# Turning part of the normed rows by transposing transfers, and moving steps of the opening, in a fused attention and SwiGLU kernel

## The chip, the cores and the metric

The kernel runs on one core of one Trainium2 chip. The metric is the device time of one execution in microseconds. Before the change it is 336.01 us, the median of 3 runs (335.22 to 336.15). A core has five engines with a queue of their own each: TensorE (PE; weight loads are shown as PEld), VectorE (DVE), ScalarE (ACT), GpSimd (POOL) and SyncE (SP), which here only issues transfers.

## The reference

Attention with a hash mask, then a SwiGLU block on its output:

```python
q_bucket, k_bucket = ...   # 6 sign bits of q @ proj and k @ proj
scores = where(q_bucket == k_bucket, q @ k.T / sqrt(64), -1e9)
attn = softmax(scores) @ v                       # 4 batches, 8 heads, 768 tokens, 64 columns
x = attn, heads side by side                     # 3072 rows of 512
xn = x / sqrt(mean(x * x, axis=-1) + 1e-6) * rms_g
g = xn @ w_gate                                  # 512 x 1536
out = (g * sigmoid(g) * (xn @ w_val)) @ w_out    # 1536 x 512
```

## The kernel before, in words

**Slots.** The work is written out by hand as 192 slots (`SLOTS`). A slot is one pair of score blocks: a half batch `w` (0 to 7, 384 queries), a head `h`, and a third `p` of the keys. Half batches 0 and 1 are the two halves of batch 0, and so on. In each slot `s` the program writes the scores of slot `s + 1` (L344), the exponential of these (L354, ACT), and whatever `at(slot, step, ..., rank=)` has put into slot `s`, lower ranks first; ranks under 3 come ahead of the exponential. This order is the order of every engine's queue: nothing is rearranged later. An engine waits at an instruction until its operands are there, and what is behind it waits too.

**Attention.** Loads of k, q and v come in pairs of heads `(b, hp)` into one pool of buffers (`lpool`, L62). The rows of k and q have to be turned so that the 64 columns lie on partitions. The pairs in `BY_PE` (batch 0 and pair (1, 0)) are turned by TensorE (`keep_pair`, L170, with a copy out of PSUM, L178); the others by VectorE in 32 x 32 blocks (`turn_dve`, L194), for which the k and q loads are cut into pieces of 32 columns (`load_blocks`, L122). Casts to fp16 follow (L186, L202). A hash (`hash_one`, `hash_pair`, `hash_lone`, `hash_pairs`; L210) makes sign bits (L217), which are moved below the turned rows in tile QK, by VectorE (L250, L270) or by SP's transfers (L248, L268, L285, L303). Scores need rows and bits. Probabilities times v are L366 (`av`), in two halves in the second and third slot after the head's last one. v is copied by `v_prep` (L310); its mean (`v_mean`, L325) is added to the output (L381). The output is normed with the reciprocal of its sum (L386, L390).

**SwiGLU.** For each half batch `w`: the squares are summed (L402, L406), `norm(w)` (L413 to L419) gives the factor `rstd`, `scale_x(w, c)` (L424, VectorE) scales chunk `c` of 128 rows, and `turn_x(w, c)` turns it: four transposes on TensorE into one PSUM bank (L431), then a product on VectorE with the gain column `gcol` into `xnT` (L432). Gates (L446), values (L456) and the output product (L469) follow: gates of `w` start at slot `s0 = 24 * w + 42`, the output products at `s0 + 16`. `bank` hands out three PSUM banks in turn to all of this: hash, turns, means, gates, values and outputs.

**SP's queue.** SP issues almost all loads, bit moves and outputs in program order. Each of its transfers also waits until the one eight places earlier has landed.

Of the kernel before, what the change touches and what calls it, by code (L numbers as in the profile page):

```python
# [8 lines left out]
FP32 = mybir.dt.float32  # L9
FP16 = mybir.dt.float16  # L10
AF = mybir.ActivationFunctionType
ALU = mybir.AluOpType
# [6 lines left out]
DMODEL = H * D  # L19
# [18 lines left out]
LAST = {(w, h): g for g, (w, h, p) in enumerate(SLOTS) if p == 2}  # L38
# [2 lines left out]
BY_PE = [(0, hp) for hp in range(4)] + [(1, 0)]  # L41


@with_exitstack
def kernel(
    ctx: ExitStack,
# [11 lines left out]
    nc = tc.nc  # L58
    PSUM = bass.MemoryType.PSUM

    const = ctx.enter_context(tc.tile_pool(name="const", bufs=1))
    lpool = ctx.enter_context(tc.tile_pool(name="lpool", bufs=10))  # L62
    tpool = ctx.enter_context(tc.tile_pool(name="tpool", bufs=2))
    qkpool = ctx.enter_context(tc.tile_pool(name="qkpool", bufs=6))
    ppool = ctx.enter_context(tc.tile_pool(name="ppool", bufs=3))
# [17 lines left out]
    scl = const.tile([128, 1], FP32, name="scl")  # L83
    mhalf = const.tile([128, 3], FP32, name="mhalf")
    gcol = const.tile([128, 4], FP32, name="gcol")
    wg = const.tile([128, 4, DFF], FP16, name="wg")
    wv = const.tile([128, 4, DFF], FP16, name="wv")
    wo = const.tile([128, NF, DMODEL], FP16, name="wo")
# [4 lines left out]
    def bank(name, shape=None, dt=FP32):  # L93
        return gps.tile(shape or [128, 512], dt, name=name, tag="g")
# [237 lines left out]
    x, ssp, xn, xnT, ht = {}, {}, {}, {}, {}  # L332
# [76 lines left out]
    rstds = {}  # L409
# [11 lines left out]
    def scale_x(w, c):  # L421
        if w not in xn:
            xn[w] = npool.tile([128, 3, DMODEL], FP16, name="xn")
        nc.vector.tensor_scalar_mul(xn[w][:, c, :], x[w][:, c, :], rstds[w][:, c : c + 1])  # L424

    def turn_x(w, c):
        if w not in xnT:
            xnT[w] = npool.tile([128, 4, HALF], FP16, name="xnT", bufs=2)
        ps = bank("x_ps", [128, 4, 128], FP16)
        for kt in range(4):  # L430
            nc.tensor.transpose(ps[:, kt, :], xn[w][:, c, kt * 128 : (kt + 1) * 128], ident16)  # L431
        nc.vector.tensor_mul(  # L432
            xnT[w][:, :, c * 128 : (c + 1) * 128], ps,
            gcol.unsqueeze(2).to_broadcast([128, 4, 128]),
        )
# [89 lines left out]
    def load_wo(f0, f1):  # L525
# [2 lines left out]
            in_=moe_w_out[f0 * 128 : f1 * 128, :].rearrange("(k p) n -> p k n", p=128),  # L528
        )

    def columns_of_proj():
        rows = pn.unsqueeze(1).to_broadcast([128, 4, 6])
        for t, sign in ((pk, 1.0), (pq, -1.0)):
            nc.vector.scalar_tensor_tensor(
                out=t[:, 0:24].rearrange("p (c n) -> p c n", n=6), in0=pm, scalar=sign,
                in1=rows, op0=ALU.mult, op1=ALU.mult,
            )
# [14 lines left out]
    keep(nc.scalar, 0, 0, "q")  # L552
    cast_half(0, 0, "q", 0, nc.scalar)
    columns_of_proj()
    idle(wz[:, 0:128], 5)
    bits0 = hash_head(0)
# [19 lines left out]
    def at(s, f, *a, rank=3):  # L576
        plan[s].append((rank, len(plan[s]), lambda: f(*a)))
# [17 lines left out]
        at(1 + h, cast_half, 0, h, "q", 1)  # L595
        at(h, (bits0, bits1)[h], (nc.vector,), 3)

    for hp, turns, sv in ((1, (1, 2, 4, 5), 8), (2, (7, 8, 9, 10), 17), (3, (12, 13, 14, 15), 22)):
        for i, s in enumerate(turns):
            at(s, keep_pair, 0, hp, i)  # L600
            at(s + 1, casts, 0, hp, i)
        at(sv, v_prep, 0, hp)

    for h, s in ((2, 3), (3, 7)):
        at(s, hash_one, h)
        for t in range(3):
            at(s + 1 + t, lambda h=h, t=t: moves[h]((nc.vector,), t), rank=5)
    for hp, s, slots in ((2, 12, (13, 14, 15, 16)), (3, 17, (18, 19, 20, 21))):
        at(s, hash_pair, 0, hp)
        for i, s in enumerate(slots):  # L610
            at(s, lambda hp=hp, i=i: moves[0, hp](nc.vector, [divmod(i, 2)]), rank=5)
    for hp, s in enumerate((6, 16, 22, 29)):
        at(s, v_mean, 0, hp, 2, range(6))
    for i, (t, src) in enumerate(((wg, moe_w_gate), (wv, moe_w_val))):
        at(2 + 4 * i, load_w, t, src, 0, 768)
        at(12 + 9 * i, load_w, t, src, 768, 1536)
        at(31 + 21 * i, load_wo, 6 * i, 6 * i + 6)


    for which, sl in zip("kqv", (9, 11, 15)):  # L620
        at(sl, load_rows, nc.sync, 1, 0, which)
    for i, sl in enumerate((23, 25, 27, 29)):
        at(sl, keep_pair, 1, 0, i)
        at(sl + 1, casts, 1, 0, i)
    at(31, hash_pair, 1, 0)
    at(27, v_prep, 1, 0)
    for h in range(2):
        at(41 + h, cast_half, 1, h, "q", 0)
# [4 lines left out]
    def in_row(loads, s, hash_slot=None):  # L633
        return loads, range(s, s + 8), (s + 4, s + 8, s + 9), hash_slot

    work = {
        (1, 1): in_row((21, 22, 32), 42, 51), (1, 2): in_row((32, 33, 37), 49, 58),
        (1, 3): in_row((38, 40, 44), 56, 65),
        (2, 0): in_row((53, 55, 58), 64), (2, 1): in_row((59, 62, 66), 72, 81),
        (2, 2): in_row((68, 71, 75), 81), (2, 3): in_row((78, 82, 86), 89, 98),  # L640
        (3, 0): in_row((90, 94, 98), 100), (3, 1): in_row((100, 104, 108), 110, 119),
        (3, 2): in_row((116, 120, 124), 126), (3, 3): in_row((126, 130, 134), 136, 145),
    }
    for (b, hp), (loads, turns, cast_slots, sh) in work.items():
        for which, s in zip("kqv", loads):
# [11 lines left out]
        at(cast_slots[2], v_sum, b, hp)  # L657
        if b > 1 and hp % 2:
            at(48 * b + (17 if hp == 3 else -4), v_mean, b, hp - 1, 4)
    for hp, s in enumerate((48, 62, 69, 78)):  # L660
        at(s, v_mean, 1, hp, 2)

    gts, sqs = {}, {}
# [13 lines left out]

    for w in range(8):
        for h in range(H):
            end = LAST[w, h] + 3  # L680
            at(end - 1, av, w, h, 0, 9)
            at(end, av, w, h, 9, 18)
            if h % 2:
                at(end, o_step, w, h // 2, rank=4.5)
                if (w, h) != (0, 7):
                    late = 3 if h == 7 and w < 3 else 5 if (w, h) == (0, 5) else 4
                    at(end + late, s_step, w, h // 2, rank=5 if late != 5 else 4)
        s0 = 24 * w + 42
        n0 = {0: 9, 2: 7}.get(w, 11)
        at(s0 - n0, norm, w, rank=5)  # L690
        for c in range(3):
            at(s0 - {0: 5 - c // 2, 2: 6 - c}.get(w, 8 - c), scale_x, w, c, rank=5)
            xs = {0: (3, 2, 1), 2: (4, 2, 1)}.get(w, (5, 3, 1))
            at(s0 - xs[c], turn_x, w, c, rank=1)
        seen = set()
        for ft in range(NF):
            for f, s in ((g_step, s0 + 16 * ft // NF), (v_step, s0 + (32 * ft + 16) // (2 * NF))):
                at(s, f, w, ft, rank=4 if s in seen else 2)
                seen.add(s)
        for i in range(9 if w < 7 else 6):  # L700
            c, j = divmod(i, 3)
            at(s0 + 16 + i, project, w, c, 4 * j, 4 * j + 4, rank=1 if i == 8 else 3)


    for s in range(NS + 48):
# [3 lines left out]
        n = sum(r < 3 for r, _, _ in todo) if s < NS - 1 else 0  # L709
# [54 lines left out]
```

## Time and profile before

| | |
|---|---|
| median of 3 runs | 336.01 us |
| profiled execution | 334.87 us, span 333.1 us |
| granted TensorE clock | 0.999 |
| busy: PE / DVE / ACT / POOL | 324.1 / 237.9 / 207.8 / 155.6 us |
| DMA | 31.36 MB, 94 GB/s on average |

The profile shows one execution. A row of a timeline has the start, the time until the end of the last of the merged instructions, the engine, the line, the operation, the tiles written and read, the number of instructions merged, and in brackets how long the engine was idle before and what ended that. `SPq` are issues of transfers on SP: their time is that of the issue, waits between them included, not that of the transfer. Matmuls are pipelined: the distance from one start to the next is what they cost.

### The profile page before, as it was taken

The page shows a single profiled execution, that of the slowest core. Times are in us where ns is not written, and L with a number is a line of the kernel's source. Part 1 is how long each engine was busy: PE and PEld are TensorE (multiplying, and loading weights), DVE is VectorE, ACT ScalarE, POOL GpSimd, SP SyncE. Part 2 cuts the span into 40 slices and gives each one's busy share as a digit, 9 for nine tenths or more (in the row PEclk, how much of TensorE's full clock was granted, in tenths as well). Part 3 has the DMA queues.
Part 4 walks back from the last instruction along what each step waited for, and adds up shares of the span by engine and source line. Part 5 has one row for each costly group of instructions (what it writes and reads, how often), then busy time and mean ns, then how long its engine had stood idle before and what let it go on. Part 6 is the DMA issues. An engine that isn't in the chain of part 4 may idle for free.

```text
span 333.1 us, 7797 instructions
## 1 busy us (share of the span) xinstructions
PE 324.1 (97%) x2983; PEld 199.3 (60%) x2983; DVE 237.9 (71%) x532; ACT 207.8 (62%) x324; POOL 155.6 (47%) x230
## 2 busy tenths in 40 slices
PE   8999989999989999999999999999999999999995
PEld 6566666555556556565566656566666656655653
DVE  4789669998588976789577785967357753793860
ACT  3789887665566666657576766657666766422421
POOL 5888955587666665737644364643110311130000
PEclk9999999999999999999999999999999999999999
DMA  7999999887649528308240751000100001002002
GB/s 218 355 229 207 159 138 147 146 143 104 138 83 171 100 49 213 46 18 153 102 81 15 147 128 63 3 16 4 65 33 0 3 31 65 2 1 83 13 0 94
DMA packets 85972, 31.36 MB, mean 94 GB/s; under 512 B 71480, under 2 KB 82992, under 8 KB 85936
## 3 DMA queue, kind: packets, MB, share of 16 engines
q1 hardware_dynamic: 82000, 26.09, 34.3%
q0 software_dynamic: 3712, 4.72, 8.8%
q8 instruction: 23, 0.38, 0.5%
q14 instruction: 13, 0.11, 0.1%
q10 hardware_dynamic: 224, 0.07, 0.1%
HBM read 28.32 MB, written 6.29 MB: 104 GB/s over the span
## 4 chain that ended last, share of the span: by engine, by line
PE 83%; DVE 7%; DMA 4%; POOL 2%; ACT 1%; issue 1%; SPq 0%; DVEq 0%; POOLq 0%; ACTq 0%
PE y_ps L469 18%; PE v_ps L456 16%; PE s_ps L344 15%; PE g_ps L446 14%; PE o_ps L366 8%; PE d_ps L210 4%; PE s_ps L446 4%; DMA wo<-in_moe_w_out_dram 2%; DMA QK<-bits 2%; PE x_ps L431 1%; PE t_ps L170 1%; PE z_ps L337 1%; PE y_ps L721 1%; DVE t L457 1%; DVE otmp L381 1%
## 5 line engine op out<-in xcount | busy, mean ns | idle before, releaser
L354 ACT ACTIVATE psb<-s_ps 128x768 f16<-128x768 f32 x192 | 150.6, 809 | 29.6 <-PE s_ps L344 27.9
L344 PE MATMUL s_ps<-QK 76*128 76x384 f16 x384 | 93.6, 325 | 2.2 <-ACT psb L354 0.9
L456 PE MATMUL v_ps<-xnT,wv 128*128 128x384 f16 x384 | 78.1, 326 | 0.0
L469 PE MATMUL y_ps<-wo,ht 128*128 128x512 f16 x276 | 69.4, 379 | 0.1
L448 ACT ACTIVATE t<-g_ps 128x384 f32<-128x384 f32 x78 | 38.2, 490 | 46.3 <-PE g_ps L446 45.7
L366 PEld LDWEIGHTS <-psb 128*128 128x128 f16 x1152 | 52.2, 97 | 21.8 <-issue 3.7
L457 DVE SCALAR_TENSOR_TENSOR t<-t,g_ps 128x384 f32<-128x384 f32 x78 | 42.7, 547 | 31.0 <-ACT t L448 30.4
L446 PE MATMUL g_ps<-xnT,wg 128*128 128x384 f16 x312 | 63.4, 325 | 1.2 <-DVE xnT L432 0.6
L390 POOL TENSOR_TENSOR x<-otmp,rcp 128x384 f32<-128x384 f32 x31 | 25.9, 835 | 79.3 <-DVE rcp L386 78.8
L458 DVE SCALAR_TENSOR_TENSOR ht<-t,v_ps 128x384 f16<-128x384 f32 x96 | 53.2, 554 | 10.5 <-PE v_ps L456 1.1
L366 PE MATMUL o_ps<-vl,psb 128*128 128x65 f16 x1152 | 56.7, 193 | 0.0
L446 PEld LDWEIGHTS <-wg 128*128 128x128 f16 x384 | 36.0, 97 | 25.1 <-issue 1.7
L456 PEld LDWEIGHTS <-wv 128*128 128x128 f16 x384 | 36.2, 97 | 23.4 <-issue 0.3
L344 PEld LDWEIGHTS <-QK 76*128 76x128 f16 x384 | 31.4, 98 | 19.9 <-issue 6.8
L469 PEld LDWEIGHTS <-ht 128*128 128x128 f16 x276 | 25.8, 97 | 25.1 <-issue 1.6
L476 ACT COPY ysb<-y_ps 128x512 f32<-128x512 f32 x23 | 13.5, 586 | 25.3 <-PE y_ps L469 24.9
L402 POOL TENSOR_TENSOR sq<-x 128x384 f32<-128x384 f32 x31 | 25.7, 828 | 2.5
L202 POOL CAST QK<-qT 64x768 f16<-64x768 f32 x22 | 18.2, 827 | 18.0 <-DVE qT L194 17.3
L432 DVE TENSOR_TENSOR xnT<-x_ps,gcol 128x512 f16<-128x512 f16 x24 | 16.2, 681 | 14.2 <-PE x_ps L431 14.2
L381 DVE TENSOR_TENSOR otmp<-o_ps,cvb 128x390 f32<-128x390 f32 x32 | 17.9, 558 | 8.2 <-PE o_ps L366 8.1
L202 POOL CAST QK<-kT 64x768 f16<-64x768 f32 x22 | 18.2, 828 | 10.5 <-PE v_ps L456 4.0
L194 DVE STREAM_TRANSPOSE kT<-kL 128x192 f32<-128x192 f32 x44 | 22.1, 517 | 0.0
(80 smaller groups left out, 300.0 us busy)
## 6 DMA issues: line engine op xcount, KB each, us to landing
vL<-in_v_dram SPq DMA_DIRECT2D x16, 384.0 KB
out_dram<-ysb SPq DMA_DIRECT2D x23, 256.0 KB
kL<-in_k_dram SPq DMA_DIRECT2D x44, 96.0 KB
qL<-in_q_dram SPq DMA_DIRECT2D x44, 96.0 KB
kL<-in_k_dram SPq DMA_DIRECT2D x4, 384.0 KB
qL<-in_q_dram SPq DMA_DIRECT2D x4, 384.0 KB
wg<-in_moe_w_gate_dram POOLq DMA_DIRECT2D x2, 768.0 KB, 8.6
wv<-in_moe_w_val_dram POOLq DMA_DIRECT2D x2, 768.0 KB, 9.1
```

What stands on the lines that cost most here:

```text
L202: nc.gpsimd.tensor_copy(QK[b, hp][0:64, hh, o : o + S], T0[b, hp, which][64 * hh : 64 * hh + 64, :])
L344: nc.tensor.matmul(ps[:, j, 0:HALF], k_cols(w // 2, h, 2 * p + j), q_cols(w, h), start=True, stop=True,)
L354: nc.scalar.activation(psb[w, h][:, p], sps.pop(g)[:, :, 0:HALF], AF.Exp, scale=ESCALE,)
L366: nc.tensor.matmul(o[:, c, hh, 0:65], psb[w, h][:, jt // 2, jt % 2, 128 * c : 128 * c + 128], vls[b % 2][:, h, v_chunk(b, h, jt), 0:65], s ...
L390: eng.tensor_mul(xd.rearrange("p c (h d) -> p c h d", h=2), tmp[:, :, :, 0:64], r.to_broadcast([128, 3, 2, 64]),)
L402: nc.gpsimd.tensor_mul(sq, xd, xd)
L446: nc.tensor.matmul(g, wg[:, kt, fs], xnT[w][:, kt], start=(kt == 0), stop=(kt == 3))
L448: nc.scalar.activation(t, g, AF.Tanh, scale=0.5)
L456: nc.tensor.matmul(vv, wv[:, kt, fs], xnT[w][:, kt], start=(kt == 0), stop=(kt == 3))
L457: nc.vector.scalar_tensor_tensor(out=t, in0=t, scalar=1.0, in1=g, op0=ALU.add, op1=ALU.mult)
L458: nc.vector.scalar_tensor_tensor(out=ht[w][:, ft], in0=t, scalar=0.5, in1=vv, op0=ALU.mult, op1=ALU.mult)
L469: nc.tensor.matmul(y, ht[w][:, ft, c * 128 : (c + 1) * 128], wo[:, ft, :], start=(ft == 0), stop=(ft == NF - 1),)
```

## The change

Two things are changed together.

First, the turning of the normed rows. For half batches 3, 4 and 5 and chunks 0 and 1 of the three, `turn_x` no longer uses TensorE. Four transposing transfers on SP write the turned blocks straight from `xn` to `xnT`. As no VectorE product follows, `scale_x` multiplies by the gain too, from a new tile `grow`, the gain broadcast to all partitions, which one load at slot 78 fills. Scaling and transfers of these chunks are put at slots `s0 - 9` and `s0 - 8`; the third chunk is turned as before. For the new tile `lpool` has 9 buffers instead of 10.

Second, slots. In the opening: head 3's k is turned at slot 3 instead of 4, the hash of head 2 at 4 instead of 3, the turns of pair (1, 0) at 20, 21, 24, 27 instead of 23, 25, 27, 29, its hash at 33 instead of 31, the last mean of batch 0 at 30 instead of 29. For half batch 0, the last head's `av` and what follows it come one slot earlier, the norm two, the scalings at `s0 - 6`, and the turns one earlier. Later: loads of (1, 2), (2, 0) to (2, 2), (3, 1) and (3, 3) and two means of batch 1 are moved.

```diff
+BY_DMA = (3, 4, 5)
-    lpool = ctx.enter_context(tc.tile_pool(name="lpool", bufs=10))
+    lpool = ctx.enter_context(tc.tile_pool(name="lpool", bufs=9))
+    grow = const.tile([128, DMODEL], FP32, name="grow")
 ...
     def scale_x(w, c):
-        nc.vector.tensor_scalar_mul(xn[w][:, c, :], x[w][:, c, :], rstds[w][:, c : c + 1])
+        if w in BY_DMA and c < 2:
+            nc.vector.scalar_tensor_tensor(
+                out=xn[w][:, c, :], in0=x[w][:, c, :], scalar=rstds[w][:, c : c + 1],
+                in1=grow, op0=ALU.mult, op1=ALU.mult,
+            )
+        else:
+            nc.vector.tensor_scalar_mul(xn[w][:, c, :], x[w][:, c, :], rstds[w][:, c : c + 1])
 
     def turn_x(w, c):
+        if w in BY_DMA and c < 2:
+            for kt in range(4):
+                nc.sync.dma_start(
+                    out=xnT[w][:, kt, c * 128 : (c + 1) * 128],
+                    in_=xn[w][:, c, kt * 128 : (kt + 1) * 128], transpose=True,
+                )
+            return
 ...
+    def load_grow():
+        nc.sync.dma_start(
+            out=grow, in_=moe_rms_g.rearrange("(o n) -> o n", o=1).to_broadcast([128, DMODEL])
+        )
 ...
-    for hp, turns, sv in ((1, (1, 2, 4, 5), 8), (2, (7, 8, 9, 10), 17), (3, (12, 13, 14, 15), 22)):
+    for hp, turns, sv in ((1, (1, 2, 3, 5), 8), (2, (7, 8, 9, 10), 17), (3, (12, 13, 14, 15), 22)):
-    for h, s in ((2, 3), (3, 7)):
+    for h, s in ((2, 4), (3, 7)):
-    for hp, s in enumerate((6, 16, 22, 29)):
+    for hp, s in enumerate((6, 16, 22, 30)):
         at(s, v_mean, 0, hp, 2, range(6))
+    at(78, load_grow)
-    for i, sl in enumerate((23, 25, 27, 29)):
+    for i, sl in enumerate((20, 21, 24, 27)):
         at(sl, keep_pair, 1, 0, i)
-    at(31, hash_pair, 1, 0)
+    at(33, hash_pair, 1, 0)
 ...
     work = {
-        (1, 1): in_row((21, 22, 32), 42, 51), (1, 2): in_row((32, 33, 37), 49, 58),
+        (1, 1): in_row((21, 22, 32), 42, 51), (1, 2): in_row((34, 35, 37), 49, 58),
-        (2, 0): in_row((53, 55, 58), 64), (2, 1): in_row((59, 62, 66), 72, 81),
-        (2, 2): in_row((68, 71, 75), 81), (2, 3): in_row((78, 82, 86), 89, 98),
-        (3, 0): in_row((90, 94, 98), 100), (3, 1): in_row((100, 104, 108), 110, 119),
-        (3, 2): in_row((116, 120, 124), 126), (3, 3): in_row((126, 130, 134), 136, 145),
+        (2, 0): in_row((53, 55, 59), 64), (2, 1): in_row((66, 67, 68), 72, 81),
+        (2, 2): in_row((71, 74, 77), 81), (2, 3): in_row((78, 82, 86), 89, 98),
+        (3, 0): in_row((90, 94, 98), 100), (3, 1): in_row((99, 101, 112), 110, 119),
+        (3, 2): in_row((116, 120, 124), 126), (3, 3): in_row((126, 127, 137), 136, 145),
     }
 ...
-    for hp, s in enumerate((48, 62, 69, 78)):
+    for hp, s in enumerate((48, 60, 64, 78)):
         at(s, v_mean, 1, hp, 2)
 ...
-            end = LAST[w, h] + 3
+            end = LAST[w, h] + (2 if (w, h) == (0, 7) else 3)
 ...
-        n0 = {0: 9, 2: 7}.get(w, 11)
+        n0 = {0: 11, 2: 7}.get(w, 11)
         at(s0 - n0, norm, w, rank=5)
         for c in range(3):
-            at(s0 - {0: 5 - c // 2, 2: 6 - c}.get(w, 8 - c), scale_x, w, c, rank=5)
-            xs = {0: (3, 2, 1), 2: (4, 2, 1)}.get(w, (5, 3, 1))
-            at(s0 - xs[c], turn_x, w, c, rank=1)
+            scale, rank = {0: 6, 2: 6 - c}.get(w, 8 - c), 1
+            turn = {0: (4, 3, 2), 2: (4, 2, 1)}.get(w, (5, 3, 1))[c]
+            if w in BY_DMA and c < 2:
+                scale, turn, rank = 9 - c, 9 - c, 6
+            at(s0 - scale, scale_x, w, c, rank=5)
+            at(s0 - turn, turn_x, w, c, rank=rank)
```

## The prediction

> **What bounds the kernel now.** I read the page's shares first, then busy time by stretches of the span.
>
> ```profile
> span 333.1 us, 7797 instructions
> PE 324.1 (97%) x2983; PEld 199.3 (60%) x2983; DVE 237.9 (71%) x532; ACT 207.8 (62%) x324; POOL 155.6 (47%) x230
> ```
> ```profile
> 28.00:32.00 4.00, 3.44 (x50) 2.34 (x47) 3.78 (x9) 3.49 (x6) 2.87 (x6) 1.00 1.02 230
> 38.00:42.00 4.00, 3.64 (x54) 2.01 (x51) 2.69 (x7) 3.22 (x5) 3.35 (x6) 1.00 1.16 188
> 42.00:48.50 6.50, 5.64 (x83) 3.98 (x80) 4.95 (x16) 5.94 (x9) 3.15 (x5) 1.00 1.11 168
> 90.00:105.00 15.00, 14.05 (x134) 8.83 (x133) 12.86 (x30) 9.52 (x16) 7.99 (x11) 1.00 0.61 133
> 127.00:166.00 39.00, 38.86 (x358) 23.48 (x357) 30.46 (x66) 25.16 (x39) 23.10 (x32) 1.00 0.46 103
> ```
>
> The columns are stretch, length, then busy time of PE, PEld, DVE, ACT and POOL, the granted clock and the DMA share. TensorE is the bound. From 127 to 166 us it has 0.14 us of holes, at full clock. There a matmul fewer is time saved, and a late operand is time lost at once. In the opening, up to 48.5 us, holes remain, but ACT (5.94 of 6.50) and DVE (3.78 of 4.00) are nearly as full, so that not every hole can be closed. The last place with holes is 90 to 105 us. TensorE's timeline names what ended each hole, in its last bracket:
>
> ```profile
> 12.44 0.83 PE L210 MATMUL d_ps<-kT,pk 128*32 128x384 f32 x2 [0.41 <-DVE kT L178]
> 29.82 0.48 PE L344 MATMUL s_ps<-QK 76*128 76x384 f16 x2 [0.30 <-POOL QK L186]
> 31.26 0.48 PE L344 MATMUL s_ps<-QK 76*128 76x384 f16 x2 [0.26 <-ACT psb L354]
> 41.49 0.49 PE L344 MATMUL s_ps<-QK 76*128 76x384 f16 x2 [0.36 <-ACT psb L354]
> 43.64 0.48 PE L344 MATMUL s_ps<-QK 76*128 76x384 f16 x2 [0.25 <-ACT psb L354]
> 48.49 0.81 PE L446 MATMUL g_ps<-xnT,wg 128*128 128x384 f16 x4 [0.58 <-DVE xnT L432]
> 94.43 0.81 PE L446 MATMUL g_ps<-xnT,wg 128*128 128x384 f16 x4 [0.47 <-DVE t L457]
> 96.56 0.48 PE L344 MATMUL s_ps<-QK 76*128 76x384 f16 x2 [0.39 <-DMA QK<-bits]
> ```
>
> The profiled execution took 334.87 us (span 333.1), the median of the runs is 336.01, so 1.14 us above it. I make the sum against 334.87 and add 1.14 at the end.
>
> **1. Opening: hash of head 2 from slot 3 to 4, the turn of head 3's k from 4 to 3.** The hash is the matmul at 12.44 that waited 0.41 us for VectorE's copy. Now a turn and a score pair stand ahead of it, work that was to be done anyway. I take 0.4 us.
>
> **2. First norm.** The second half of head 7's probabilities times v comes one slot earlier, the norm two, the three scalings at slot 36 instead of 37, 37 and 38, the turns one slot earlier each; the hash of (1, 0), whose matmuls stood ahead of this chain, goes behind it. The gate's wait of 0.58 us goes. Price: nothing new is issued, and the norm's small operations find POOL waiting for VectorE:
>
> ```profile
> 43.49 0.19 POOL L415 TENSOR_SCALAR ms<-ss 128x3 f32<-128x3 f32 x1 [2.08 <-DVE ss L413]
> ```
>
> I take 0.6 us.
>
> **3. Turns of (1, 0) to slots 20, 21, 24, 27 and its hash to 33.** They put TensorE work into slots in which it waited for ACT or POOL (0.30, 0.26, 0.36 and 0.25, together 1.17 us) and take it out of fuller ones. ACT must keep up:
>
> ```profile
> 40.63 7.36 ACT L354 ACTIVATE psb<-s_ps 128x768 f16<-128x768 f32 x10 [0.36 <-PE s_ps L344]
> ```
>
> From 40.63 to 48 it runs ten exponentials with no pause, at 0.73 us each ((7.36 - 0.81)/9 with a last one of 0.81), so that part can't be shortened, only be entered earlier; the pause ahead of it, 0.36, and ACT's share of 3.49 in 4.00 before 32 us leave room. I take half of the 1.17: 0.6 us; bounds 0 and 1.2. Two k casts on POOL now come ahead of the copy of v of (0, 3); its mean is one slot later for that. Opening together: 1.6 us (0 to 2.2).
>
> **4. Second stage, 90 to 105 us.** The 0.47 at 94.43 follows the mean of (1, 2) at slot 69, which holds one of three PSUM banks in the middle of gates; it moves to slot 64, ahead of them. The 0.39 at 96.56 is a wait for bits. Their signs were ready at 86.42, but on SP they stood behind loads and an output:
>
> ```profile
> 85.74 0.68 DVE L217 TENSOR_SCALAR bits<-d_ps,thr,scl 128x384 f16<-128x384 f32 x1
> ...
> 99.47 0.54 DVE L194 STREAM_TRANSPOSE kT<-kL 128x192 f32<-128x192 f32 x1
> ```
> ```profile
> 85.89 2.85 SPq L122 DMA_DIRECT2D kL<-in_k_dram  x4
> 88.84 0.58 SPq L478 DMA_DIRECT2D out_dram<-ysb  x1
> 89.47 2.67 SPq L122 DMA_DIRECT2D qL<-in_q_dram  x4
> 92.91 7.05 SPq L285 DMA_DIRECT2D QK<-bits  x8
> ```
>
> The change puts those k and q loads at slots 66 and 67, behind the bits, which can then go at 86.4 instead of 92.9. What is late next: these loads themselves. Bits to about 93.5 (7.05 us), an output 0.58, k 2.85, then 1.84 of landing (row below) is 98.8; VectorE needs the k rows at 99.47 less what is gained before, which moves SP's start as well. So the margin is some tenths. I take 0.8 of the 0.86.
>
> The eight other moved loads and the pool of nine buffers instead of ten cost nothing: the tile nine places back is read some slots ahead of each load, with one exception, the load of v of (0, 3) in the opening, which now waits for the turn of head 3's k (near 12 us) on SP; its v is needed near slot 22. The broadcast load of the gain (256 KB, once, at slot 78) is one more SP issue, some 0.5 us, ahead of a k load due eleven slots later.
>
> **5. Turns by transfers, w = 3, 4, 5.** Removed from TensorE: 3 x 2 x 4 = 24 transposes. Their price is the distance of starts:
>
> ```profile
> 157.25 0.39 PE L431 MATMUL x_ps<-ident,xn 128*128 128x128 f16 x4
> 157.48 1.03 PE L469 MATMUL y_ps<-wo,ht 128*128 128x512 f16 x4
> ```
>
> Four take 0.23 us (their 218 ns each overlap), so six groups take 1.4 us, in a stretch without holes. I take 1.3, with what may be hidden. VectorE loses six of these products (the first row) and gets six scalings with the gain in a two-input form, like the third row:
>
> ```profile
> L432 DVE TENSOR_TENSOR xnT<-x_ps,gcol 128x512 f16<-128x512 f16 x24 | 16.2, 681 | 14.2 <-PE x_ps L431 14.2
> L424 DVE TENSOR_SCALAR xn<-x,rstd 128x512 f16<-128x512 f32 x24 | 15.4, 668 | 2.9 <-POOL rstd L419 2.9
> L458 DVE SCALAR_TENSOR_TENSOR ht<-t,v_ps 128x384 f16<-128x384 f32 x96 | 53.2, 554 | 10.5 <-PE v_ps L456 1.1
> ```
>
> That is 554 x 512/384 = 739 ns instead of 668: 0.4 us more and 4.1 less, on an engine that is not the bound.
>
> Added: 24 transposing transfers on SP, 8 per half batch, between a scaling at slots s0 - 9 and s0 - 8 and the first gate at s0. The trace has no such transfer. So I work out the room and then what price fits it.
>
> ```profile
> 152.63 2.71 SPq L122 DMA_DIRECT2D qL<-in_q_dram  x4
> ...
> 190.02 2.71 SPq L122 DMA_DIRECT2D qL<-in_q_dram  x4
> 195.83 0.35 SPq L478 DMA_DIRECT2D out_dram<-ysb  x1
> ```
> ```profile
> 165.99 0.81 PE L446 MATMUL g_ps<-xnT,wg 128*128 128x384 f16 x4
> 203.97 0.81 PE L446 MATMUL g_ps<-xnT,wg 128*128 128x384 f16 x4
> 242.49 0.81 PE L446 MATMUL g_ps<-xnT,wg 128*128 128x384 f16 x4
> ```
> ```profile
> 193.08 1.02 DVE L424 TENSOR_SCALAR xn<-x,rstd 128x512 f16<-128x512 f32 x1
> ```
> ```profile
> 227.44 0.86 POOL L419 TENSOR_TENSOR rstd<-ms,mhalf 128x3 f32<-128x3 f32 x1
> ```
> ```profile
> 94.59 1.84 DMA QK<-bits
> ```
>
> For w = 3 the q load of (3, 1), now at slot 101, still ends on SP at 155.34, since SP works without pause there; the scaled rows are ready by then. The gate comes at 165.99 - 0.45 (the turns that are gone); its fourth matmul, which needs the last transfer, 0.49 later. So 165.99 - 0.45 + 0.49 - 155.34 = 10.7 us of room. For w = 4: 203.97 + 0.04 - 192.73 = 11.3 (the first scaling, at 193.08 before, is a slot earlier and done near 192.8: 11.2). For w = 5, SP is idle, the norm is ready at 227.44 + 0.86 = 228.3 and the scaling done near 229.6: 12.9. With a landing of 1.84 us, as in the last row, eight transfers at x us each (by SP's issue or by the queue, whichever is slower) fit when 8x + 1.84 is under 10.7: x up to 1.11 us. Each tenth above costs 0.8 us per half batch.
>
> Nearest rows for x: an output of 128 rows takes 0.35 us of SP, a k load of 32 partitions with 768 short pieces 2.85/4 = 0.71, a bit row 7.05/8 = 0.88. From below 0.35. From above nothing is certain: pieces at 2.71/(4 x 768) = 0.88 ns each, an estimate, would make 16,384 single elements 14.4 us. A turned block of 128 rows has to be cut finer than an output, but no reason in the trace makes it elementwise; I take the price near the short-piece load, 0.7 to 0.9, so 8x + 1.84 is 7.4 to 9.0 us and no gate waits. SP's next work, the outputs of the half batch before and the loads of v, is late by at most some us, and three output buffers cover that until the next half batch, 24 slots on.
>
> The Trainium skill, VectorE: DVE Perf Modes, section The three transpose paths, lists 390 ns for TensorE and 1309 ns for the transfer of a 128 x 128 block. By its 390 the removed turns would be worth 24 x 0.39 = 9.4 us; the starts above say 1.4. If its 1309 is what each costs in a row, x is above the limit: waits of 1.6 and 1.1 us, and the sum 335.0 instead of 332.3. Its page Advanced Engine Details and Errata, section X-Bar Transpose (TRN2), says instead that such transfers are as fast as plain ones, which is the forecast. No row here decides between them.
>
> **Sum.** 334.87 - 1.6 - 0.8 - 1.3 = 331.2; with 1.14 it is 332.3, said as 332.4.
>
> **Rivals.**
> - *Transfers a little dear.* x of 1.11 to 1.42. SP's dearest four loads took 1.4 us each, while DMA was full:
>
> ```profile
> 36.37 5.50 SPq L122 DMA_DIRECT2D qL<-in_q_dram  x4
> ```
>
> At 1.41 the waits at the three gates are 2.4, 1.9 and 0.2 us, together 4.5: 336.8. In the middle 335.
> - *Transfers dear: slower.* One mechanism: PE stands at the first gate of w = 3, 4 and 5 for the last transfer. From x = 1.42 us the three waits exceed 4.7 us and eat all gains; at 2 us they are 7.1, 6.6 and 4.9 and the time is 351. For it: the trace shows no transfer that turns, and the scaling was put nine slots ahead. Against: every SP row but those with full rings is under 0.9 us.
> - *The moved slots give nothing.* ACT and DVE at 90% and more take the opening's holes back, and VectorE waits at slot 72 for the late k rows: only step 5 is left, 336.01 - 1.3 = 334.7, up to 336.5 with waits of that kind.
>
> **Chances.** A difference under 0.3% (1.0 us) can hardly be told from none here. Forecast 0.48 (331 to 334); a little dear 0.13 (0.06 faster, 0.04 same, 0.03 slower); dear 0.20, slower; slots give nothing 0.19 (0.07 faster, 0.07 same, 0.05 slower). Faster 0.61, same 0.11, slower 0.28. The range goes from 330.8, all holes named closed, to 338.5, which is x near 1.5; what lies beyond is most of the dear case.
>
> **What would show it.** Right: SP's transposing issues near 0.7 to 0.9 us each and no wait of g_ps for DMA in front of w = 3, 4, 5; no 0.58 at the first gate, which starts near 46.9 instead of 48.49; no 0.47 and 0.39 near 93; 24 transposes fewer. Wrong: PE g_ps waiting for DMA xnT, or for ACT and POOL in the opening as long as before, or DVE's L194 waiting for kL near 96.

## The result, and the profile after

The changed kernel took 337.84 us, the median of 22 runs (336.84 to 339.39); before, on the same chip, took 336.22 (22 runs, 335.12 to 339.58). The ratio is 1.004, with a 95% interval of 1.0021 to 1.0059: about 1.3 us slower. The prediction said 332.4, faster; the time lies in its range, near the upper end, but on the slower side of before.

The page of after begins so (columns as before):

```profile
span 336.0 us, 7784 instructions
PE 324.2 (96%) x2959; PEld 198.1 (59%) x2959; DVE 233.7 (70%) x526; ACT 208.2 (62%) x324; POOL 156.4 (47%) x230
```

The 24 transposes are gone from TensorE (2983 to 2959), and six products from VectorE, yet the span is 2.9 us longer. Busy time by stretches says where TensorE stands:

```profile
90.00:105.00 15.00, 14.22 (x138) 9.13 (x137) 12.28 (x30) 10.05 (x18) 7.87 (x11) 1.00 0.62 121
127.00:166.00 39.00, 38.84 (x351) 23.10 (x349) 28.95 (x64) 25.17 (x39) 23.47 (x32) 1.00 0.41 84
166.00:169.00 3.00, 1.43 (x8) 0.76 (x8) 0.00 (x0) 0.96 (x2) 0.82 (x1) 1.00 0.34 113
204.00:208.00 4.00, 3.04 (x24) 1.49 (x21) 0.32 (x2) 1.13 (x3) 1.26 (x3) 1.00 0.32 101
244.00:247.00 3.00, 2.43 (x14) 1.19 (x13) 0.20 (x1) 1.30 (x3) 0.00 (x0) 1.00 0.44 156
```

The stretch from 127 to 166 us is as full as it was. Three short stretches behind it are not, and each lies at the first gate of one of the half batches 3, 4 and 5. The waits of TensorE over the whole span, longest sum first (us, times, longest):

```profile
PE g_ps L463 <- DMA xnT<-xn: 2.4, 3, 0.9
...
PE v_ps L473 <- DVE t L474: 0.8, 1, 0.8
PE g_ps L463 <- ACT ysb L493: 0.7, 1, 0.7
PE x_ps L448 <- DVE xn L434: 0.5, 1, 0.5
```

The first row is the one the prediction named as its refutation. TensorE's timeline at these gates:

```profile
166.65 0.69 PE L463 MATMUL g_ps<-xnT,wg 128*128 128x384 f16 x3 [0.68 <-ACT ysb L493]
168.26 0.32 PE L463 MATMUL g_ps<-xnT,wg 128*128 128x384 f16 x1 [0.92 <-DMA xnT<-xn]
...
207.10 0.32 PE L463 MATMUL g_ps<-xnT,wg 128*128 128x384 f16 x1 [0.90 <-DMA xnT<-xn]
...
245.91 0.34 PE L463 MATMUL g_ps<-xnT,wg 128*128 128x384 f16 x1 [0.57 <-DMA xnT<-xn]
```

A gate is four matmuls, one for each block of 128 columns; the last of them (x1) needs the last transfer, and all four need chunk 1. At 166.65 the first three had waited too. The row names ACT's copy `ysb`, which ended just then (166.01 and 0.59). The transfers didn't end this wait: by the trace's records of landings, the blocks that the first two matmuls need were there at 164.34 and 165.61. Why the gate waits for that copy stays open; in `e3_one_chunk`, with fewer transfers, and in `e4_room`, with eight, the same gate starts ahead of the same copy.

```profile
164.96 0.81 PE L463 MATMUL g_ps<-xnT,wg 128*128 128x384 f16 x4
```
```profile
165.16 0.58 ACT L493 COPY ysb<-y_ps 128x512 f32<-128x512 f32 x1 [1.80 <-PE y_ps L486]
```

For the sum it makes no difference: the fourth matmul starts at 168.26, when the last transfer has landed (168.22), whatever the first three do, so the whole delay of this gate is the transfers'. Against the usual distance of starts, TensorE loses 2.0, 1.3 and 0.7 us at the three gates, 4.0 in all. The other side is SP's timeline:

```profile
152.89 2.71 SPq L126 DMA_DIRECT2D qL<-in_q_dram  x4
155.79 11.28 SPq L441 DMA_TRANSPOSE xnT<-xn  x8
167.17 1.00 SPq L495 DMA_DIRECT2D out_dram<-ysb  x2
...
191.38 3.26 SPq L126 DMA_DIRECT2D qL<-in_q_dram  x4
195.25 10.71 SPq L441 DMA_TRANSPOSE xnT<-xn  x8
...
233.93 10.80 SPq L441 DMA_TRANSPOSE xnT<-xn  x8
```

and, of the transposing line alone, the shortest, median and longest issue in ns:

```profile
L441 SPq DMA_TRANSPOSE xnT<-xn x24: 1094/1230/2165, 155.8 to 243.5; - x24
```

One issue takes 1.23 us, and eight in a row 10.7 to 11.3, 1.34 to 1.41 each: in every row one issue takes 1.9 to 2.2 us, for which I have no explanation, and pauses between issues add the rest. The prediction's limit was 1.11.

Where along the kernel the time goes is worked out from the starts of the score matmuls (L348): the start of a slot's scores, minus the same in the profile of before, in us.

| slot | 44 | 72 | 80 | 96 | 191 (the last) |
|---|---|---|---|---|---|
| after | -0.27 | -1.02 | -0.01 | +0.27 | +2.94 |
| without transfers (`e1_no_transfers`, below) | -0.36 | -1.58 | -0.28 | -0.01 | -0.02 |
| one chunk by transfer (`e3_one_chunk`, below) | -0.11 | -1.19 | -1.08 | -0.81 | -1.46 |

At slot 112 after is still even with before (+0.05). It is at +1.78 in slot 120, +2.64 in slot 144 and +2.94 from slot 168 on: the steps are the first gates of half batches 3, 4 and 5. The table also warns: by the ends of the profiles, `e1_no_transfers` gains nothing, while by the runs below it gains 1.9 us. The one profiled execution of before was a good one (334.87 us, where the medians of its four series lie at 335.34 to 336.59), so gains under 2 us are judged by the repeated runs here, and profiles are used for places and durations.

### The profile page after: what moved, and what is told of

It reads as the page before. It is cut to its first block, busy times and chain, and to the rows that moved or that the text cites. A ratio compares the mean times of both kernels' runs of the same rounds, so it can differ in the third digit from the quotient of the medians.

```text
span 336.0 us, 7784 instructions
## 1 busy us (share of the span) xinstructions
PE 324.2 (96%) x2959; PEld 198.1 (59%) x2959; DVE 233.7 (70%) x526; ACT 208.2 (62%) x324; POOL 156.4 (47%) x230
## 4 chain that ended last, share of the span: by engine, by line
PE 70%; SPq 8%; DMA 8%; DVE 7%; POOL 3%; ACT 2%; issue 2%; DVEq 0%; POOLq 0%; ACTq 0%
PE v_ps L473 16%; PE g_ps L463 12%; PE s_ps L348 12%; PE y_ps L486 12%; PE o_ps L370 7%; SPq L441 4%; PE s_ps L463 3%; SPq L289 3%; PE d_ps L214 3%; DMA xnT<-xn 3%; DMA wo<-in_moe_w_out_dram 2%; DMA QK<-bits 1%; DMA kL<-in_k_dram 1%; DVE kT L198 1%; PE t_ps L174 1%
## 5 line engine op out<-in xcount | busy, mean ns | idle before, releaser
L348 PE MATMUL s_ps<-QK 76*128 76x384 f16 x384 | 93.8, 325 | 1.6 <-ACT psb L358 0.8
L463 PE MATMUL g_ps<-xnT,wg 128*128 128x384 f16 x312 | 64.1, 325 | 3.5 <-DMA xnT<-xn 2.4
L475 DVE SCALAR_TENSOR_TENSOR ht<-t,v_ps 128x384 f16<-128x384 f32 x96 | 53.2, 554 | 10.5 <-PE v_ps L473 0.9
L348 PEld LDWEIGHTS <-QK 76*128 76x128 f16 x384 | 31.3, 98 | 18.4 <-issue 4.8
L198 DVE STREAM_TRANSPOSE qT<-qL 128x192 f32<-128x192 f32 x44 | 21.8, 515 | 0.0
```

Source lines behind the costliest of these rows:

```text
L198: nc.vector.transpose(dst.rearrange("p (c t r) -> p r c t", c=6, r=4)[:, r : r + 1], src.rearrange("p (r c) d -> p r c d", r=4)[:, r : r + 1],
L348: nc.tensor.matmul(ps[:, j, 0:HALF], k_cols(w // 2, h, 2 * p + j), q_cols(w, h), start=True, stop=True,)
L463: nc.tensor.matmul(g, wg[:, kt, fs], xnT[w][:, kt], start=(kt == 0), stop=(kt == 3))
L475: nc.vector.scalar_tensor_tensor(out=ht[w][:, ft], in0=t, scalar=0.5, in1=vv, op0=ALU.mult, op1=ALU.mult)
```

## The experiments

All ratios are to before on the same chip, with 95% intervals; a ratio isn't always the quotient of the two medians, and where they differ I go by the ratio; before's median was 336.59 us (13 runs) with the first four kernels below (`e1` to `e4`), 336.46 (35 runs) with `e5`, `e6`, `e7` and `e9`, and 335.34 (18 runs) with `e8` and `e10` to `e12`.

**Which of the two things costs.** The theory: the transfers hold TensorE at three gates and cost more than the slots gain. The rival: the moved slots cost (late k rows, the longer queue in front of bits) and transfers are innocent.

```diff
-BY_DMA = (3, 4, 5)
+BY_DMA = ()
```

> The changed kernel with all chunks of half batches 3 to 5 turned by TensorE again; all moved slots, the gain row's load and the nine buffers stay. Theory P (the 24 transfers take SP 1.23 us each, and the gates' waits for them, 1.9 + 1.3 + 0.7 us, less 1.3 us of transposes, are the loss): 2.6 us under the changed kernel in the profile, so 0.1 to 0.6 us from the kernel before, span near 333.3. Rival S (the moved slots or the smaller pool cost by themselves): stays over 1 us above the kernel before.

334.88 us (333.69 to 335.75), ratio 0.9944 (0.9924 to 0.9964), -1.9 us. All of the loss is the transfers': with what they save on TensorE counted in, they cost 1.004 - 0.9944 = 0.96%, 3.2 us. The rival falls.

The other half alone, on before:

```diff
+BY_DMA = (3, 4, 5)
...
-    lpool = ctx.enter_context(tc.tile_pool(name="lpool", bufs=10))
+    lpool = ctx.enter_context(tc.tile_pool(name="lpool", bufs=9))
...
+            if w in BY_DMA and c < 2:
+                scale, turn, rank = 9 - c, 9 - c, 6
...
-        (3, 0): in_row((90, 94, 98), 100), (3, 1): in_row((100, 104, 108), 110, 119),
-        (3, 2): in_row((116, 120, 124), 126), (3, 3): in_row((126, 130, 134), 136, 145),
+        (3, 0): in_row((90, 94, 98), 100), (3, 1): in_row((99, 101, 112), 110, 119),
+        (3, 2): in_row((116, 120, 124), 126), (3, 3): in_row((126, 127, 137), 136, 145),
```

The gain row, the two-input scaling and the transfers are as in the change.

> The kernel before with the transfers for half batches 3 to 5, the gain row, nine buffers and the moved loads of (3, 1) and (3, 3); opening and second stage as before. Theory P: 2 to 3 us slower than the kernel before, three waits of the first gates for xnT. Rival S: within 1 us of the kernel before. If both parts had only partial shares, about 1.5 us slower here.

339.73 us (339.28 to 340.78), ratio 1.0099 (1.0079 to 1.012): +3.3 us, by medians 3.1, the same as the difference above. TensorE's waits in its profile:

```profile
PE g_ps L461 <- DMA xnT<-xn: 2.6, 4, 0.9
PE s_ps L346 <- DMA QK<-bits: 2.3, 3, 1.1
```

The first row is the transfers'. The second, waits for bits, was 0.4 in the profile of before and changes from profile to profile; it lies in the second stage, ahead of all transfers.

**Is it the number of transfers, and the room?** If a gate waits because eight issues take 11 us, then four issues, or eight that start earlier, must cure it. If the transfers hurt in another way (the mode itself, the DMA engines, SP's later work), neither would cure it fully. Four per half batch:

```diff
-        if w in BY_DMA and c < 2:
+        if w in BY_DMA and c < 1:
```

The same line is changed in `scale_x`, in `turn_x` and where the slots are given.

> The changed kernel with chunk 0 alone turned by transfers, four per half batch instead of eight; chunk 1 by TensorE at s0 - 3. Theory P: four take 5 us of SP, no gate waits for them, 12 transposes fewer are worth 0.7 us: 0.7 us under the run without transfers, span near 332.6. Rival (a transfer has a price beside SP's issue, in DMA or memory): no gain over the run without transfers.

333.58 us (333.12 to 334.58), ratio 0.9914 (0.9894 to 0.9933), -2.9 us. SP's transposing issues:

```profile
155.79 5.25 SPq L441 DMA_TRANSPOSE xnT<-xn  x4
192.80 5.78 SPq L441 DMA_TRANSPOSE xnT<-xn  x4
230.04 4.95 SPq L441 DMA_TRANSPOSE xnT<-xn  x4
```

About the same price each (1.24 to 1.45 us), half as many, and TensorE has no wait between 150 and 250 us. Eight, started earlier:

```diff
-        (3, 0): in_row((90, 94, 98), 100), (3, 1): in_row((99, 101, 112), 110, 119),
-        (3, 2): in_row((116, 120, 124), 126), (3, 3): in_row((126, 127, 137), 136, 145),
+        (3, 0): in_row((90, 94, 98), 100), (3, 1): in_row((96, 97, 112), 110, 119),
+        (3, 2): in_row((116, 117, 124), 126), (3, 3): in_row((118, 118, 137), 136, 145),
...
-                    late = 3 if h == 7 and w < 3 else 5 if (w, h) == (0, 5) else 4
+                    late = 3 if h == 7 and w < 6 else 5 if (w, h) == (0, 5) else 4
...
-        n0 = {0: 11, 2: 7}.get(w, 11)
+        n0 = {0: 11, 2: 7}.get(w, 12 if w in BY_DMA else 11)
...
-                scale, turn, rank = 9 - c, 9 - c, 6
+                scale, turn, rank = 10 - c, 10 - c, 6
```

> The changed kernel, still eight transfers per half batch, with more room: loads of k and q of (3, 1) and (3, 3) ahead of the bit transfers in SP's queue, sums of squares, norm, scaling and transfers of half batches 3 to 5 one slot earlier. Theory P: the transfers start 1.5 to 3 us earlier, so the waits of 1.9 and 1.3 us go and the 0.7 goes too or shrinks; 24 transposes fewer are worth 1.3 us: span near 332, under the run without transfers. If instead the price of a transfer grows with what stands beside it, waits of over 1 us stay.

334.14 us (333.2 to 334.38), ratio 0.9924 (0.9906 to 0.9942).

```profile
153.81 11.19 SPq L441 DMA_TRANSPOSE xnT<-xn  x8
191.82 10.95 SPq L441 DMA_TRANSPOSE xnT<-xn  x8
229.77 10.74 SPq L441 DMA_TRANSPOSE xnT<-xn  x8
```

The eight take as long as in after and start 2.0, 3.4 and 4.2 us earlier by the clock. As TensorE is late in after by then, this is less against the gates: 1.7, 1.4 and 1.0 us. That is just enough. The fourth matmul of the first two gates still comes 0.17 and 0.19 us late, and at the third it is on time; nothing else is left of the 4.0 us. So it is the start and the length of the row of issues, against the gate. That speaks against a cost of the mode itself; the next run asks this directly. In the next edit the rows are turned by TensorE, and the 24 transfers are issued as well, into a tile that nobody reads:

```diff
-BY_DMA = (3, 4, 5)
+BY_DMA = ()
+COPIES = (3, 4, 5)
...
+            aside[w] = npool.tile([128, 4, 256], FP16, name="aside", bufs=1)
+        for kt in range(4):
+            nc.sync.dma_start(
+                out=aside[w][:, kt, c * 128 : (c + 1) * 128],
+                in_=xn[w][:, c, kt * 128 : (kt + 1) * 128], transpose=True,
+            )
...
+            if w in COPIES and c < 2:
+                at(s0 - scale, turn_aside, w, c, rank=6)
```

> The run without transfers, with the 24 transfers added for nothing: from the scaled rows into a tile that nobody reads, at the slots of the scaling; TensorE does all turns. Theory P (a transfer costs time only where a gate waits for it, or where SP's later work is late): within 0.5 us of the run without transfers, SP issues of 1.2 us each. Rival: 1 us slower or more, if the transfers hinder loads, outputs or VectorE.

334.81 us (333.49 to 338.57), ratio 0.9939 (0.9909 to 0.9968), against 0.9944 without any transfer.

```profile
155.60 10.45 SPq L461 DMA_TRANSPOSE aside<-xn  x8
193.56 10.98 SPq L461 DMA_TRANSPOSE aside<-xn  x8
230.46 11.27 SPq L461 DMA_TRANSPOSE aside<-xn  x8
```

24 transfers at the full price, at nearly the same places, cost nothing measurable (the intervals leave room for some tenths of a per cent) when nobody waits for them. SP's work behind them (outputs, loads of v) has the slack that the prediction gave it.

**The slots, part by part.** Opening alone, on before:

```diff
-    for hp, turns, sv in ((1, (1, 2, 4, 5), 8), (2, (7, 8, 9, 10), 17), (3, (12, 13, 14, 15), 22)):
+    for hp, turns, sv in ((1, (1, 2, 3, 5), 8), (2, (7, 8, 9, 10), 17), (3, (12, 13, 14, 15), 22)):
-    for h, s in ((2, 3), (3, 7)):
+    for h, s in ((2, 4), (3, 7)):
-    for hp, s in enumerate((6, 16, 22, 29)):
+    for hp, s in enumerate((6, 16, 22, 30)):
-    for i, sl in enumerate((23, 25, 27, 29)):
+    for i, sl in enumerate((20, 21, 24, 27)):
-    at(31, hash_pair, 1, 0)
+    at(33, hash_pair, 1, 0)
...
-            end = LAST[w, h] + 3
+            end = LAST[w, h] + (2 if (w, h) == (0, 7) else 3)
-        n0 = {0: 9, 2: 7}.get(w, 11)
+        n0 = {0: 11, 2: 7}.get(w, 11)
```

The scalings and turns of half batch 0 are moved as in the change.

> The kernel before with the moved slots of the opening alone (hash of head 2, turns and hash of pair (1, 0), last head, norm, scalings and turns of half batch 0), ten buffers. The prediction: 1.6 us faster. Theory D (the two casts that now stand earlier on POOL hold back the squares of (0, 2), VectorE's queue waits 1.4 us for their sum, and the norm's chain starts hardly earlier): 0 to 0.6 us faster, a wait of x_ps for the scaled rows of about 0.5 us in place of the gate's 0.58.

338.07 us (336.24 to 339.36), ratio 1.003 (1.0 to 1.0061): not a gain of 1.6 us, rather a loss, though the interval touches no change. TensorE's waits, and SP's timeline behind the hash:

```profile
PE s_ps L344 <- DMA QK<-bits: 3.4, 3, 1.8
```
```profile
43.08 8.40 SPq L122 DMA_DIRECT2D kL<-in_k_dram  x4
51.58 6.20 SPq L268 DMA_DIRECT2D QK<-bits  x8
```

The hash of (1, 0), moved from slot 31 to 33, has fallen behind the k load of (1, 2) at slot 32 in SP's queue: its bits go out at 51.58 instead of 41.97. The change as a whole has those loads at 34 and 35. A theory follows (Q): the hash and these loads are one step that must move together. The opening with these loads moved along:

```diff
-        (1, 1): in_row((21, 22, 32), 42, 51), (1, 2): in_row((32, 33, 37), 49, 58),
+        (1, 1): in_row((21, 22, 32), 42, 51), (1, 2): in_row((34, 35, 37), 49, 58),
```

> The opening alone again, with the k and q loads of (1, 2) two slots later (34, 35), behind the bits of (1, 0) whose hash the opening moves from slot 31 to 33. Theory Q (in the opening alone the bits of (1, 0) stood behind those loads on SP, left at 51.6 us instead of 42 to 46, all later SP work was late by that, and TensorE waited 3.1 us for bits near 76 and 95): the waits for bits fall to what the kernel before has, time 0.3 to 0.8 us under it. Rival (the opening itself disturbs the second stage): stays about 1 us above it.

334.74 us (334.1 to 336.4) against 335.34, ratio 0.9977 (0.9955 to 0.9999). The bits go out in time again:

```profile
43.42 8.14 SPq L268 DMA_DIRECT2D QK<-bits  x8
```

From 1.003 to 0.9977 by two loads placed two slots later; the two intervals lie side by side. The opening is worth 0.8 us, with an interval that nearly reaches no change.

The second stage alone, on before:

```diff
-        (1, 1): in_row((21, 22, 32), 42, 51), (1, 2): in_row((32, 33, 37), 49, 58),
+        (1, 1): in_row((21, 22, 32), 42, 51), (1, 2): in_row((34, 35, 37), 49, 58),
-        (2, 0): in_row((53, 55, 58), 64), (2, 1): in_row((59, 62, 66), 72, 81),
-        (2, 2): in_row((68, 71, 75), 81), (2, 3): in_row((78, 82, 86), 89, 98),
+        (2, 0): in_row((53, 55, 59), 64), (2, 1): in_row((66, 67, 68), 72, 81),
+        (2, 2): in_row((71, 74, 77), 81), (2, 3): in_row((78, 82, 86), 89, 98),
-    for hp, s in enumerate((48, 62, 69, 78)):
+    for hp, s in enumerate((48, 60, 64, 78)):
```

> The kernel before with the moved loads of (1, 2), (2, 0), (2, 1), (2, 2) and the two moved means alone. The prediction: 0.8 us faster. By the run without transfers (1.9 us faster with opening and second stage together): 1.3 to 1.9 us faster if the opening gives 0 to 0.6, by shorter waits for bits; VectorE waits 1 to 2 us for the k rows of (2, 1). If that wait counted in full: no gain.

335.59 us (334.65 to 338.11), ratio 0.9972 (0.9938 to 1.0007): -0.9 us, near the 0.8 taken, but the interval holds no change too.

**What the late rows and the norm cost.** In after VectorE waits 1.92 us for the k rows of (2, 1), and a value behind it on TensorE 0.78:

```profile
100.52 0.53 DVE L198 STREAM_TRANSPOSE kT<-kL 128x192 f32<-128x192 f32 x1 [1.92 <-DMA kL<-in_k_dram]
```
```profile
101.90 0.32 PE L473 MATMUL v_ps<-xnT,wv 128*128 128x384 f16 x1 [0.78 <-DVE t L474]
```

Beside four transfers per half batch (the edit of the run above with one chunk), these rows were loaded two slots earlier:

```diff
-        (2, 0): in_row((53, 55, 59), 64), (2, 1): in_row((66, 67, 68), 72, 81),
+        (2, 0): in_row((53, 55, 59), 64), (2, 1): in_row((64, 67, 68), 72, 81),
```

> The run with one chunk by transfers, with the k load of (2, 1) at slot 64, ahead of the bits of (1, 3) on SP, instead of 66. Theory: VectorE's wait of 1 to 2 us for these k rows goes, TensorE's wait for VectorE behind it (0.3 to 1.1 us) goes, the bits start 2 us later and still come in time: 0.3 to 0.8 us under the run with one chunk, and less scatter. If the bits come late: TensorE waits for them near 95 us and nothing is gained.

332.86 us (332.32 to 334.15) against 335.34, ratio 0.9913 (0.9881 to 0.9944). VectorE's wait is gone, and the ratio is that of `e3_one_chunk` (0.9914), not the 0.3 to 0.8 us less that were expected. It can't settle the matter: the intervals are as wide as the wait. In the profiles the late rows do cost. In the seven kernels that load them at slot 66 (after, `e1`, `e3`, `e4`, `e6`, `e7` and `e9`), VectorE waits 1.0 to 2.2 us for them in all seven, and TensorE 0.3 to 1.1 us behind it in six; only in the profile of `e3_one_chunk`, where VectorE waits 1.0, TensorE doesn't. Between slots 72 and 80 after gives back 1.0 us and `e1_no_transfers` 1.3 of what the second stage had gained; `e8_k_ahead` gives back nothing.

The norm: in after the gate's 0.58 has become a wait of the turn ahead of it for the scaling, and the first gate starts at 48.22, 0.27 earlier than before. VectorE's timeline shows what stands ahead of it:

```profile
40.23 0.56 DVE L410 TENSOR_REDUCE ssp<-sq 128x3 f32<-128x384 f32 x1 [1.41 <-POOL sq L406]
40.70 0.55 DVE L385 TENSOR_TENSOR otmp<-o_ps,cvb 128x390 f32<-128x390 f32 x1
42.87 0.17 DVE L417 TENSOR_REDUCE ss<-ssp 128x3 f32<-128x12 f32 x1
44.42 1.28 DVE L434 TENSOR_SCALAR xn<-x,rstd 128x512 f16<-128x512 f32 x3 [0.77 <-POOL rstd L423]
```

The sum of the squares of an earlier pair stands in VectorE's queue ahead of the last pair's output (`otmp`), and waits 1.41 us for POOL's squares. A theory (D): let the sum go behind that output, and the chain starts 1.4 us earlier.

```diff
-                    at(end + late, s_step, w, h // 2, rank=5 if late != 5 else 4)
+                    at(end + late, s_step, w, h // 2, rank=5 if late != 5 else 4.8)
```

> The run with one chunk by transfers, with the sum of squares of (0, 2) behind the output of (0, 3) in VectorE's queue instead of ahead of it (rank 4.8 instead of 4). Theory D: VectorE no longer waits for POOL's squares ahead of the norm, the chain to the first gate starts about 1 us earlier, the wait of x_ps goes: 0.4 to 0.8 us under the run with one chunk. If ACT's chain of exponentials is the opening's bound: no difference.

On `e3_one_chunk`: 333.97 us (333.04 to 335.75), ratio 0.9916 (0.9887 to 0.9945), no gain. In its profile VectorE's wait is gone and the output starts at 39.32 instead of 40.70, but its product with the reciprocal takes 1.14 us instead of 0.56, and the sum (0.54) now stands between the last square and the final sum: `ss` starts at 42.72 instead of 42.87. The theory's cure falls; what would bring the first norm forward stays open.

**All together.** The room of `e4_room`, the sum behind, and the k rows early:

> The changed kernel with the room of the run with early loads (eight transfers per half batch), the sum behind, and the k load ahead. The transfers' gates don't wait: 24 transposes fewer give 1.3 us, the k load 0.5: 332.5 to 333.5, ratio to the kernel before 0.988 to 0.991. If eight transfers still wait: no better than the run with one chunk.

333.06 us (331.83 to 334.84), ratio 0.9919 (0.9887 to 0.995), just short of the expected 0.988 to 0.991. And the same with a fourth half batch:

```diff
-BY_DMA = (3, 4, 5)
+BY_DMA = (3, 4, 5, 6)
...
-                    late = 3 if h == 7 and w < 6 else 5 if (w, h) == (0, 5) else 4
+                    late = 3 if h == 7 and w < 7 else 5 if (w, h) == (0, 5) else 4
```

> As the run with all, and half batch 6 turned by transfers too (32 transposes fewer instead of 24). SP is idle there: 0.4 us less again, ratio 0.987 to 0.990. If the scaled rows of half batch 6 come too late for eight issues of 1.2 us: a wait at its first gate and no gain.

332.57 us (332.15 to 333.91) against 335.34, ratio 0.9906 (0.9873 to 0.9938): the fastest by ratio, by medians 2.8 us better than before. Its transfers start within 0.7 us of those of `e4_room`, and the fourth eight has room as well:

```profile
265.23 10.03 SPq L441 DMA_TRANSPOSE xnT<-xn  x8
```

The first two gates lose 0.07 and 0.13 us, the other two nothing. Its interval overlaps those of the other cured kernels (0.9913 to 0.9924), so which of them is best isn't settled; that each beats both before and after is.

## Why the prediction was wrong

**Step 5's price failed.** The prediction took 0.7 to 0.9 us for one transposing transfer; it is 1.23, and 1.34 to 1.41 in a row of eight. The room was nearly right. From SP's start to the time at which the gate's fourth matmul would have started, the trace gives 10.5, 10.5 and 11.2 us, where 10.7, 11.2 and 12.9 had been worked out. With its own room, the prediction's rival "a little dear" at 1.41 said waits of 2.4, 1.9 and 0.2 us; TensorE lost 2.0, 1.3 and 0.7. The first two are shorter because the last landing took less than the 1.84 of the bits: at half batch 3 the last issue ended at 167.07 and the matmul started at 168.26, so 1.2. The third is longer because the scaling came late. By then after is 2.6 us behind, so that 229.6 becomes 232.2, but VectorE only starts it at 232.80:

```profile
232.80 1.77 DVE L429 SCALAR_TENSOR_TENSOR xn<-x,rstd,grow 128x512 f16<-128x512 f32 x2
```

At half batches 3 and 4 too, the first transfer starts when the first scaling ends (155.76 and 195.18; SP starts at 155.79 and 195.25), a little after the q load is through (155.60 and 194.64).

Instead of the -1.3 us taken for step 5 it was +3.2. By the prediction's own terms the waits eat the 3.7 us of gains at 1.37 us a transfer, and not only at 1.42 as it says, so the price measured is just about that border. Where I chose wrongly: of the near rows, I placed the turned block beside the 768-piece load, without a row that turns anything, though the limit of 1.11 was only a quarter above the value taken and the result hung on it 24 times.

The Trainium skill's page VectorE: DVE Perf Modes, section The three transpose paths, gives 1309 ns for such a transfer; the trace agrees within 6%, with a median issue of 1230 ns, and the prediction's sentence on it, with 335.0, had the right mechanism and too little of it. Its 390 ns for TensorE isn't what a block costs here: taking 24 away with 0.4 us of new waits (`e4_room` against `e1_no_transfers`) gave 0.002 of 336, 0.7 us, not 9.4. The two intervals overlap, and `e4_room` moves other slots as well, but 9.4 us is far outside them. The Trainium skill's page Advanced Engine Details and Errata, section X-Bar Transpose (TRN2), on which the forecast leaned in that sentence, says as fast as plain transfers; an output of 128 rows is issued in 0.35 us, so for the issue it doesn't hold here.

**The gain of the turns** isn't resolved. 1.3 was taken for 24 transposes; the ratios give 0.7 for 24 (`e4_room`), 1.0 for 12 (`e3_one_chunk`, 0.9944 to 0.9914) and 0.4 for 8 more (`e11_four`, 0.9919 to 0.9906). In each case the intervals overlap. That some gain exists is likely, its size stays open.

**Steps 1 to 3, the opening.** Taken 1.6; measured 0.8 by `e12_opening_loads`. The interval of that run holds both nearly nothing and nearly all of it. The profiles say little: in ten of the eleven kernels that have the opening, 0.4 to 0.7 us are gained from slot 4 to slot 44. Step 2 failed as put: the gate's 0.58 went, but the first gate came at 48.22 and not near 46.9, as the wait moved to the turn (0.49). The order on VectorE's queue was overlooked, but it isn't the whole reason: without the sum's wait for POOL (`e7_sum_behind`) the chain starts only 0.15 earlier. Step 3 failed as well: from 20 to 50 us TensorE's waits for ACT are 0.8 us in after and were 0.9 before; the wait for POOL is gone, but three small ones have come, so that all waits there sum to 1.9 us, where they were 1.8. Step 1 is seen at slot 8 as 0.65 us gained from slot 4 on; by slot 24, 0.4 of it is left in after and nothing in `e12_opening_loads`. The prediction counted the loads of (1, 2) among "the eight other moved loads" that cost nothing (there are twelve). They matter: the hash's move alone is rather a loss, and these loads, placed behind it, turn it into a gain.

**Step 4, the second stage.** Taken 0.8, measured 0.9 alone, with an interval that holds no change too. The waits of 0.47 and 0.39 are gone, and the bits went out ahead of the loads, as predicted:

```profile
87.38 6.09 SPq L289 DMA_DIRECT2D QK<-bits  x8
94.08 2.76 SPq L126 DMA_DIRECT2D kL<-in_k_dram  x4
```

but the margin of the k rows, "some tenths", was short by 1.92 us. SP was done with them at 96.84, as worked out (96.9). They were there at 100.52 only, 3.7 us later, where I had taken 1.84, the landing of a bit row, for a load of 3072 short pieces. This was named as a sign of being wrong, and it gave back 0.8 us on TensorE in after (0 to 1.1 in the other profiles).

**The slots together**: taken 2.4, measured 1.9 (`e1_no_transfers`; its two parts alone 0.8 and 0.9). The rival "the moved slots give nothing" falls. **The other moved loads and the smaller pool**: no cost of theirs is seen in `e1_no_transfers`, which has them all and gains. **VectorE's two-input scaling**, taken as 739 ns, took 1.77 us for two in the row above (0.89 each).

The two parts measured apart add up to the whole: 336.2 - 1.9 (`e1_no_transfers`) + 3.3 (`e2_transfers_alone`) = 337.6, against 337.84 measured.

## What to carry to other kernels

Work taken off the bounding engine is worth only what comes back before its due time: price the new issue, times its count, on its in-order queue, and compare that with the room; where the room is 10.7 us and the rows bound the price of eight only from below, at 3, measure the price first or move half as much. Moving a step in an in-order queue moves its distance to every neighbour: the hash moved by two slots was rather a loss (1.003) until two loads moved with it (0.9977). And where waits scatter from execution to execution, the difference of two profiled spans can hide or invent 2 us (`e1_no_transfers` and before: spans 333.0 and 333.1, medians 334.88 and 336.59); take places from the profile and verdicts from repeated runs.

## What was unexpected in the hardware

The transposing transfers are bound by their issue, not by the moving. While SP issued the eight of half batch 3, the DMA engines (last but one column) were busy only 0.23 of the time:

```profile
155.80:167.10 11.30, 10.62 (x96) 5.99 (x95) 5.83 (x13) 6.56 (x10) 8.30 (x11) 1.00 0.23 39
```

By the packet records of one transfer, its 128 packets of 256 B start when the issue ends and move within 0.3 us, and completion is written 0.4 to 0.5 us later, while the issue takes 1.23. The next issue mostly starts within 0.05 us of the end of the one before, without waiting for these packets. The price in SP's queue hardly depends on what else runs: the median is 1.23 us in every kernel with 24 or 32 such transfers, two or three of them take 1.9 to 2.4, and eight take 10.0 to 11.3 us in every place.
